# A decode step of attention plus a bilinear GLU: three filler matmuls taken out, a fourth one shortened

## The chip, the cores and the metric

The kernel runs on one core of one Trainium2 chip. The metric is the device time of one execution in microseconds; lower is better. A measurement is the median of several executions, and beside it stands one execution taken by the hardware profiler, from which all the rows below come.

## The reference

One token for each of two batch entries (B = 2, D = 512) goes through a layer norm, and then through two branches whose results are added to the input:

```python
W = min(4096, max(256, Sk // 4))            # 2048 of 8192 cached positions
q = (x @ wq).reshape(B, Sq, Hq, Dh)         # 32 heads of 128, Sq = 1
scores = einsum("bhqd,bhkd->bhqk", q, k) * Dh ** -0.5
o = einsum("bhqk,bhkd->bhqd", softmax(scores), v)
A = o.reshape(B, Sq, Hq * Dh) @ wo
Bm = ((x @ w_gate) * (x @ w_up)) @ w_down   # F = 1376, no nonlinearity
return x + A + Bm                           # x in A and Bm is the normed input
```

All is fp32. The last 2048 positions of the two caches are 32 heads x 2 x 2048 x 128 x 2 x 4 bytes = 134 MB, and every weight is read once too; the profile counts 159.5 MB of reads.

## The kernel before, in words

The host lays all inputs out in one stream, in the order in which the kernel uses them. `blocks()` writes that order down: a first small load, then steps of up to 31 x 512 columns by 128 partitions. A step goes by one DMA into one of three buffers (`BUFS = 3`, tile `step`). `pump()` issues the next load as soon as one of the buffers is free, and `done()` counts down the fields of a buffer and calls `pump()` when the last one has been used. All loads are issued on SyncE (SP). The last ones are smaller. One holds the keys of head 31, the values of head 28 with their rows of `wo`, and two blocks of `w_down` (4864 KB). The next two go into one buffer: the values of head 29 with half of those of head 31, `vh 0` (3328 KB), and the values of head 30 (2304 KB). The last four go into another buffer: the other half of head 31's values, `vh 1` (1024 KB); `wo` of head 31 with three blocks of `w_down` (1024 KB); one block of `w_down` and three half blocks (640 KB); and the last half block (128 KB). A load is told as landed as a whole.

A head h goes through these steps, each on the engines named:

- `products(h)`: VectorE multiplies the keys (128 x 8192 in two batch entries, 4096 in each access) by the query, in place in the buffer.
- `sums(h)`: VectorE sums them into the scores; then `maxima(h)` on VectorE and GpSimd.
- `weights(h)`: ScalarE takes the exponentials; GpSimd sums them over the partitions. `reciprocals(h)` on VectorE.
- `pv([h])`: TensorE multiplies the weights `p` with the values in the buffer, into the PSUM tile `o_ps`, in four groups of columns; ScalarE copies the result into `o_sb` (`copy_out`).
- `transpose([h], o_sb)`: eight small matmuls into the PSUM tile `tr`; ScalarE scales the result into `oT`.
- `project_o(h)`: TensorE multiplies `oT` with `wo`, into the accumulator `acc`.

The order on each engine is the order in which the kernel's text issues the instructions (`InOrder` fixes it), and it is written by hand from head 28 on. `down(n)`, `down_half(c, n)` are the parts of the second matmul of the GLU and also add to `acc`. Before head 28 is projected, the accumulator is copied to SBUF once (`acc_sb`, VectorE), and `accumulate(carry, acc_sb)` puts it back into PSUM in another layout, four groups of columns wide.

In this last part stand matmuls whose result is never read. `keep_busy(n)` multiplies a constant with n columns of another constant into a spare PSUM tile, `spare`. In the loop over heads 28 and 29 there are three more, which read the products of head 29 from the buffer. In the trace all of these write the tile `q`, from whose pool `spare` is taken. In fp32 a matmul stands in the trace as two MATMUL records and two LDWEIGHTS records. The TensorE's operations go through one helper and therefore carry one line number, L126; they are told apart by their tiles and shapes.

With H = 32: `HF` is head 28, and "the sums of heads 25 to 27" of the change are the `project_o` calls of the loop over `range(H - 7, HF)`.

Of the kernel before, what the change touches and what calls it, by code (L numbers as in the profile page):

```python
# [21 lines left out]
FB = 4 * P  # L22
# [10 lines left out]
GC = HG * DH  # L33
# [108 lines left out]
def kernel(  # L142
# [27 lines left out]
    tiles, used, left, got = {}, {}, {}, {}  # L170
# [46 lines left out]
    mean_w = const.tile([P, P], F32, name="mean_w")  # L217
# [87 lines left out]
    def products(h):  # L305
        g, hh = divmod(h, HG)
        kt = k_of(h)
        qb = q_ps[g][:, :, hh * DH : (hh + 1) * DH] if h else q_first
        dve.tensor_tensor(
            kt, kt, qb.unsqueeze(2).to_broadcast([P, B, J, DH]), op=ALU.mult  # L310
        )

    def sums(h):
        s_t[h] = small.tile([P, B, J], F32, name="s")
        dve.tensor_reduce(s_t[h], k_of(h), axis=AX.X, op=ALU.add)
        done("k", h)

    def maxima(h):
        s = s_t[h]
        m = small.tile([P, B], F32, name="m")  # L320
        dve.tensor_reduce(m, s, axis=AX.X, op=ALU.max)
        mm = small.tile([P, B], F32, name="mm")
        nc.gpsimd.partition_all_reduce(mm, m, P, bass_isa.ReduceOp.max)  # L323
        mm_t[h] = mm

    def weights(h):
        s, mm = s_t.pop(h), mm_t.pop(h)
        nm = small.tile([P, B], F32, name="nm")
        act.mul(nm, mm, -SCALE)
        p_t[h] = p_ring[h % NP]  # L330
        rs = small.tile([P, B], F32, name="rs")
        for b in range(B):
            act.activation(
                p_t[h][:, b, :, 8 * side(h) + 4 * b : 8 * side(h) + 4 * b + 4],
                s[:, b, :].rearrange("p (i r) -> p i r", r=4),
                AF.Exp, bias=nm[:, b : b + 1], scale=SCALE, accum_out=rs[:, b : b + 1],
            )
        sum_t[h] = small.tile([P, B], F32, name="sum")
        nc.gpsimd.partition_all_reduce(sum_t[h], rs, P, bass_isa.ReduceOp.add)  # L339

    def reciprocals(h):
        rec_t[h] = small.tile([P, B], F32, name="rec")
        dve.reciprocal(rec_t[h], sum_t.pop(h))
# [10 lines left out]
    def keep_busy(n):  # L354
        pe.matmul(spare[:, 0:n], mean_w, spare_in[:, 0:n], start=True, stop=True)
# [42 lines left out]
    def project_o(h):  # L398
        wo = got["wo", h][0]
        if h < HF:  # L400
            pe.matmul(acc, oT.pop(h), wo, start=(h == 0), stop=False)
        else:
            accumulate(oT.pop(h), wo)
        done("wo", h)
# [114 lines left out]
    spare = ps_q.tile([P, B, GC], F32, name="q")[:, 0, :]  # L519
    for h in (H - 4, H - 3):  # L520
        products(h)
        if h == H - 3:
            for i in range(3):
                pe.matmul(
                    spare, mean_w, got["k", h][0][:, i * FB : (i + 1) * FB], start=True, stop=True
                )
        sums(h)
        maxima(h)
        weights(h)
        reciprocals(h - 1)  # L530

    h = H - 2
# [5 lines left out]
    keep_busy(256)  # L538
    for i in range(H - 7, HF):
        project_o(i)  # L540
    for n in (GC, GC, 256):
        keep_busy(n)
    maxima(h)
    reciprocals(h - 1)
    products(h + 1)
# [144 lines left out]
```

## Time and profile before

| | us |
|---|---|
| median of 3 executions | 379.3 |
| lowest, highest | 379.0, 380.2 |
| the profiled execution | 379.05 |
| its span, first to last instruction | 377.2 |
| mean granted TensorE clock in it | 0.824 |
| busy: TensorE / VectorE / ScalarE | 257.0 / 295.4 / 57.4 |
| moved by DMA: mean rate over the span | 423 GB/s |

The profiled execution lies 0.25 us below the median, and 379.05 - 377.2 = 1.85 us of it lie outside its span. Times in rows of the trace count from the start of the span. A TensorE row of the timeline merges neighbouring records of one kind; its second number reaches to the modelled end of the last one, while the start of the next row tells when the next kind began. The granted clock (PEclk) is 1.00 at full speed.

### The profile page before, as it was taken

To read this page: it belongs to the slowest core of one execution; us is meant where nothing else is said; L and a number is where in the kernel's file an instruction comes from. 1 tells how busy PE (TensorE), PEld (TensorE's weight loads), DVE (VectorE), ACT (ScalarE), POOL (GpSimd) and SP (SyncE) were. 2 spreads that over 40 slices of the span, in tenths; PEclk is the share of its full clock that TensorE was granted. 3 is DMA by queue.
4 is the path that set the end of the run, shared out by engine and by line. 5 is a ranking of instruction groups with operands and counts; after the bars stand their busy time and mean duration, and the time that the engine had idled before them with its cause. 6 is when DMAs were issued, how large, how long until landed. Compare 5 with 4: busy or idle time off the path is not lost.

```text
span 377.2 us, 2895 instructions
## 1 busy us (share of the span) xinstructions
PE 257.0 (68%) x1106; PEld 89.0 (24%) x1106; DVE 295.4 (78%) x145; ACT 57.4 (15%) x260; POOL 25.3 (7%) x74
## 2 busy tenths in 40 slices
PE   3167795888586852786768706886628674759996
PEld 3133122222222220222222202231202220223243
DVE  4069999369989379999279999793899999999550
ACT  1002011110210210021012002111100210202131
POOL 1000000001010000000000000000000000000010
PEclk9999697598586996688968955898766988679999
DMA  8999999999999999999999999999999999999993
GB/s 342 430 462 464 423 405 442 431 431 432 433 431 438 431 431 431 433 431 431 438 433 438 438 431 451 431 433 431 431 431 438 426 431 431 431 415 456 405 420 151
DMA packets 3938, 159.74 MB, mean 423 GB/s; under 512 B 441, under 2 KB 697, under 8 KB 982
## 3 DMA queue, kind: packets, MB, share of 16 engines
q1 hardware_dynamic: 3926, 159.58, 98.0%
q8 instruction: 8, 0.13, 0.1%
q14 instruction: 4, 0.03, 0.0%
HBM read 159.51 MB, written 0.07 MB: 423 GB/s over the span
## 4 chain that ended last, share of the span: by engine, by line
DMA 60%; PE 20%; DVE 18%; ACT 1%; issue 1%; SPq 0%; DVEq 0%
DMA step<-in_stream_dram 60%; DVE step L126 9%; DVE s L126 8%; PE q L126 7%; PE o_ps L126 6%; PE acc L126 4%; PE tr L126 3%; ACT o_sb L126 1%; ACT oT L126 0%; DVE m L126 0%; SPq L126 0%; DVE o_out L126 0%; DVE rec L126 0%; DVEq L126 0%
## 5 line engine op out<-in xcount | busy, mean ns | idle before, releaser
L126 DVE TENSOR_TENSOR step<-step,q 128x4096 f32<-128x4096 f32 x31 | 136.8, 4412 | 44.3 <-DMA step<-in_stream_dram 38.4
L126 DVE TENSOR_REDUCE s<-step 128x32 f32<-128x4096 f32 x32 | 141.4, 4419 | 1.1
L126 PE MATMUL o_ps<-step,p 128*16 128x512 f32 x512 | 77.3, 663 | 42.7 <-DMA step<-in_stream_dram 42.7
L126 PE MATMUL q<-step,xnb 128*128 128x512 f32 (+1 forms) x128 | 76.2, 742 | 33.6 <-DMA step<-in_stream_dram 33.6
L126 PEld LDWEIGHTS q<-step,xnb 128*128 128x128 f32 x128 | 28.9, 242 | 84.1 <-issue 68.6
L126 PE MATMUL acc<-step,oT 128*2 128x512 f32 (+1 forms) x88 | 36.3, 572 | 8.6 <-ACT oT L126 8.6
L126 PE MATMUL tr<-first,o_sb 128*128 128x2 f32 (+4 forms) x192 | 29.3, 271 | 16.9 <-ACT o_sb L126 11.8
L126 PEld LDWEIGHTS tr<-first,o_sb 128*128 128x128 f32 (+2 forms) x192 | 26.7, 213 | 42.4 <-ACT o_sb L126 35.2
L126 ACT COPY o_sb<-o_ps 128x512 f32<-128x512 f32 x23 | 13.5, 586 | 149.3 <-PE o_ps L126 149.3
L126 PEld LDWEIGHTS o_ps<-step,p 128*16 128x16 f32 x512 | 13.6, 100 | 95.3 <-DMA step<-in_stream_dram 50.1
L323 POOL PARTITION_ALL_REDUCE mm<-m x32 | 11.5, 359 | 239.4 <-DVE rec L126 137.3
L126 ACT ACTIVATE nm<-mm 128x2 f32<-128x2 f32 x32 | 6.6, 205 | 125.9 <-POOL mm L323 125.9
L339 POOL PARTITION_ALL_REDUCE sum<-rs x32 | 12.8, 400 | 100.6 <-ACT p L126 100.6
L126 ACT ACTIVATE p<-s,nm 128x16 f32<-128x16 f32 x64 | 19.2, 300 | 1.0
L126 PE MATMUL o_ps<-step,xn 128*2 128x512 f32 (+1 forms) x48 | 13.7, 630 | 5.4 <-DMA step<-in_stream_dram 5.4
L126 ACT ACTIVATE oT<-tr,rec 128x1 f32<-128x1 f32 x64 | 12.1, 260 | 27.7 <-PE tr L126 27.7
L126 DVE TENSOR_TENSOR step<-step,tr 128x4096 f32<-128x4096 f32 x1 | 4.4, 4421 | 15.0 <-DMA step<-in_stream_dram 15.0
L126 ACT ACTIVATION_READ_ACCUMULATOR p<-s,nm 128x1 f32 x64 | 11.9, 186 | 0.0
L126 PEld LDWEIGHTS acc<-step,oT 128*2 128x2 f32 x88 | 4.2, 86 | 20.7 <-ACT oT L126 12.1
L126 DVE RECIPROCAL rec<-sum 128x2 f32<-128x2 f32 x32 | 5.0, 155 | 4.9 <-POOL sum L339 4.9
L126 PE MATMUL q<-xnb,mean_w 128*128 128x512 f32 (+4 forms) x24 | 8.7, 465 | 0.0
L126 PE MATMUL q<-step,mean_w 128*128 128x512 f32 x6 | 5.5, 1083 | 4.3 <-DVE step L126 4.3
(42 smaller groups left out, 48.8 us busy)
## 6 DMA issues: line engine op xcount, KB each, us to landing
step<-in_stream_dram SPq DMA_DIRECT2D x15, 7936.0 KB, 30.9
step<-in_stream_dram SPq DMA_DIRECT2D x1, 7808.0 KB, 38.8
step<-in_stream_dram SPq DMA_DIRECT2D x1, 7680.0 KB, 20.9
step<-in_stream_dram SPq DMA_DIRECT2D x1, 7552.0 KB, 57.7
step<-in_stream_dram SPq DMA_DIRECT2D x1, 4864.0 KB
step<-in_stream_dram SPq DMA_DIRECT2D x1, 3328.0 KB, 17.7
step<-in_stream_dram SPq DMA_DIRECT2D x1, 2304.0 KB, 22.8
step<-in_stream_dram SPq DMA_DIRECT2D x2, 1024.0 KB, 15.7
```

The lines of the kernel that those rows point to most:

```text
L126: made = call(*args, **kwargs)
L323: nc.gpsimd.partition_all_reduce(mm, m, P, bass_isa.ReduceOp.max)
L339: nc.gpsimd.partition_all_reduce(sum_t[h], rs, P, bass_isa.ReduceOp.add)
```

## The change

The three `keep_busy` calls (512, 512 and 256 columns) between the projections of heads 25 to 27 and the maxima of head 30 are taken out. Of the three matmuls on head 29's products, the third has 320 columns in place of 512.

```diff
     for h in (H - 4, H - 3):
         products(h)
         if h == H - 3:
-            for i in range(3):
+            for i, n in enumerate((FB, FB, 320)):
                 pe.matmul(
-                    spare, mean_w, got["k", h][0][:, i * FB : (i + 1) * FB], start=True, stop=True
+                    spare[:, :n], mean_w, got["k", h][0][:, i * FB : i * FB + n],
+                    start=True, stop=True,
                 )
         sums(h)
         maxima(h)
...
     keep_busy(256)
     for i in range(H - 7, HF):
         project_o(i)
-    for n in (GC, GC, 256):
-        keep_busy(n)
     maxima(h)
     reciprocals(h - 1)
     products(h + 1)
```

## The prediction, as it was made before any run

> **What bounds the kernel now.** I read the page first, for the whole span.
>
> ```profile
> DMA  8999999999999999999999999999999999999993
> ```
>
> The 16 DMA engines are busy in every slice but the last, so up to some 370 us the loads set the time, and only what TensorE (PE) and VectorE (DVE) do after the last loads can be shortened. Both edits lie there. I went on to the chain that ended last, and to PE's timeline from 340 us on.
>
> ```profile
> 349.42 2.67 PE acc L126 x6
> 352.08 2.35 PE q L126 x6
> ```
>
> ```profile
> 352.01 2.42 PE L126 MATMUL q<-xnb,mean_w 128*128 128x512 f32 x6
> 354.36 1.91 PE L126 MATMUL o_ps<-step,p 128*16 128x512 f32 x16
> 356.09 1.88 PE L126 MATMUL acc<-step,hT 128*2 128x512 f32 x4
> 357.90 1.05 PE L126 MATMUL tr<-first,o_sb 128*128 128x2 f32 x8
> ...
> 359.85 0.40 PE L126 MATMUL acc<-o_sb,first 2*2 2x128 f32 x8
> ...
> 360.50 1.45 PE L126 MATMUL q<-xnb,mean_w 128*128 128x512 f32 x4
> 361.88 1.91 PE L126 MATMUL o_ps<-step,p 128*16 128x512 f32 x16
> ...
> 367.43 1.91 PE L126 MATMUL o_ps<-step,p 128*16 128x512 f32 x16
> ...
> 369.79 1.05 PE L126 MATMUL o_ps<-step,p 128*16 128x512 f32 x8
> ...
> 371.55 1.05 PE L126 MATMUL tr<-first,o_sb 128*128 128x4 f32 x8
> 372.53 0.84 PE L126 MATMUL acc<-step,hT 128*2 128x128 f32 x24
> ...
> 373.63 0.85 PE L126 MATMUL acc<-step,hT 128*2 128x128 f32 x40
> ```
>
> The chain runs through the three fillers (352.08, six records of tile q, 2.35 us) straight into the value matmuls of head 28. No row here names an idle time: from 352 to the end at 373.63 + 0.85 = 374.5 every step starts when PE is through with the one before. So the last 22 us are bound by PE, and PE does 2.35 us there for nobody. What can catch it is the loads.
>
> ```profile
> 342.12 0.33 SPq L126 DMA_DIRECT2D step<-in_stream_dram  x1
> step<-in_stream_dram SPq DMA_DIRECT2D x1, 3328.0 KB, 17.7
> 342.50 0.43 SPq L126 DMA_DIRECT2D step<-in_stream_dram  x1
> step<-in_stream_dram SPq DMA_DIRECT2D x1, 2304.0 KB, 22.8
> 352.11 0.33 SPq L126 DMA_DIRECT2D step<-in_stream_dram  x1
> step<-in_stream_dram SPq DMA_DIRECT2D x1, 1024.0 KB, 15.7
> ```
>
> These are the SyncE issues, each with the row of the DMA view that has its size and its time to landing. Head 29's values land at 342.12 + 17.7 = 359.8, head 30's at 365.3, the second half of head 31's at 352.11 + 15.7 = 367.8. Between the first two, 2304 KB took 5.5 us. By that rate the load before the first of these (head 31's keys, head 28's values) landed 3328 / 2304 x 5.5 = 7.9 us before 359.8, at 351.9, and the last three (1024, 640 and 128 KB: 2.4, 1.5 and 0.3 us) land at about 370.2, 371.8 and 372.1. These four are estimates from the three landings that the rows give. PE uses each of them about 2 us after its landing: 354.36, 361.88, 367.43, 369.79. Only those 2 us can be had.
>
> **The change, part by part.** *The three fillers out.* They are 2 x (512 + 512 + 256) columns in six records; from 352.01 to 354.36 is 2.35 us, all on PE's chain. Head 28's values (351.9) are there when the projections end at 352.0, so they start at once, at 352.05: 2.3 us earlier. `down(1)`, 356.09, comes to 353.8 and ends at 355.5. Beside it runs VectorE:
>
> ```profile
> 352.11 4.42 DVE L126 TENSOR_TENSOR step<-step,q 128x4096 f32<-128x4096 f32 x1 [2.40 <-PE acc L126]
> 358.07 0.68 DVE L126 COPY o_sb<-acc 2x512 f32<-2x512 f32 x1 [1.54 <-PE acc L126]
> 358.68 4.40 DVE L126 TENSOR_REDUCE s<-step 128x32 f32<-128x4096 f32 x1
> ```
>
> The products of head 31 start at 352.11, with the landing; the view names PE, whose projections end at the same moment, and if it is PE they come no later. They end at 356.53, and the copy of the accumulator then idles 1.54 us for `down(1)`. That stall goes: the copy runs 356.55 to 357.2, the sums of head 31 from 357.2 to 361.6, and head 31's weights come 1.45 us earlier than now. On PE the carry (359.85) would come 2.3 us earlier, at 357.5, just when the copy is there. The next fillers start at 358.1 and end at 359.3; then PE waits 0.6 us for head 29's values, and starts them at 359.9, **2.0 us earlier** than 361.88. From there everything keeps 2.0 us: head 30's values at 365.45 against a landing of 365.3, head 31's second half at 367.8 against 367.8, transposes 369.6, `down(2)` 370.55 against 370.2. Head 31's weights, needed by PE at 363.8, come within 0.1 us of it. `down(3)` and the half blocks would start at 371.65 and wait for 371.8 and 372.1; the forty records now take 373.63 to 374.5, of which those behind 371.8, some 0.85 us, and the last eight behind 372.1 remain. So PE ends at about 372.75, not 374.5: **1.75 us**. The 0.6 us between 2.35 and that are given to the loads.
>
> *The shorter filler.* Its cost is read where it runs.
>
> ```profile
> 335.55 5.46 PE L126 MATMUL q<-step,mean_w 128*128 128x512 f32 x6 [4.27 <-DVE step L126]
> 338.24 0.34 PEld L126 LDWEIGHTS q<-step,mean_w 128*128 128x128 f32 x1 [0.52 <-issue]
> 339.10 0.34 PEld L126 LDWEIGHTS q<-step,mean_w 128*128 128x128 f32 x1 [0.52 <-issue]
> ```
>
> A record of 512 columns takes 339.10 - 338.24 = 0.86 us here, where the clock is at half; 192 columns less in two records are 2 x 0.86 x 192/512 = 0.64 us. The value matmuls of heads 25 to 27 follow without a gap, so 0.64 us more of them run at half speed, and from 341.1 on PE is 0.32 us ahead. In the end this buys nothing: at 352 it is 0.3 us more of waiting for the load at 351.9. The SP issues that wait for these projections (352.11) move up 0.3 us, into a queue that needs 15.7 us to get to them. At nothing, then, as long as the clock holds; if it does not, the price is the next part's.
>
> **The clock** is the cover to doubt. The steps of the granted clock lie on a grid of 3.41 us. I asked for the grid's stretches: PE busy first, PEclk third from the end; below them the same for the transposes alone (tile tr), which stream 2 to 4 columns per record.
>
> ```profile
> 252.36:255.78 3.42, 2.21 (x15) 1.23 (x12) 3.39 (x2) 1.30 (x5) 0.00 (x0) 1.00 0.95 411
> 255.78:259.19 3.41, 3.41 (x5) 0.86 (x4) 2.12 (x3) 0.73 (x5) 0.36 (x1) 0.50 1.07 465
> 269.43:272.84 3.41, 2.49 (x11) 1.35 (x12) 3.38 (x2) 0.78 (x3) 0.00 (x0) 1.00 1.03 447
> 272.84:276.26 3.42, 2.85 (x4) 0.67 (x2) 3.39 (x4) 0.81 (x5) 0.36 (x1) 0.50 0.98 427
> 327.46:330.87 3.41, 2.52 (x12) 1.22 (x12) 3.38 (x2) 1.05 (x5) 0.00 (x0) 1.00 1.12 484
> 330.87:334.28 3.41, 0.41 (x1) 0.00 (x0) 3.41 (x3) 0.89 (x5) 0.76 (x2) 1.00 0.90 391
> 334.28:337.70 3.42, 2.15 (x3) 1.15 (x4) 3.38 (x2) 0.00 (x0) 0.00 (x0) 0.50 1.03 446
> 337.70:341.11 3.41, 3.41 (x8) 0.85 (x11) 2.98 (x4) 0.44 (x3) 0.36 (x1) 0.50 0.74 318
> 344.52:347.94 3.42, 2.92 (x29) 1.34 (x22) 3.39 (x2) 1.00 (x3) 0.00 (x0) 1.00 0.89 380
> ```
>
> ```profile
> 252.36:255.78 3.42, 1.05 (x8) 0.97 (x8) 0.00 (x0) 0.72 (x4) 1.00 0.95 411
> 269.43:272.84 3.41, 1.05 (x8) 0.97 (x8) 0.00 (x0) 0.41 (x2) 1.00 1.03 447
> 327.46:330.87 3.41, 1.06 (x8) 0.97 (x8) 0.00 (x0) 0.72 (x4) 1.00 1.12 484
> 344.52:347.94 3.42, 1.17 (x9) 1.08 (x10) 0.00 (x0) 0.41 (x2) 1.00 0.89 380
> ```
>
> Busy less transposes is 1.16 us in the stretch at 252.36, and the next one ran at 0.50. At 269.43 it is 1.44, and the next ran at 0.50 too. At 327.46 it is 1.46, and the next one still had 1.00. So with about 1.45 us of real streaming in 3.41 the clock holds. At 344.52 it is now 1.75; with PE 0.32 us ahead, 0.32 us of value matmuls leave this stretch at its front and only transposes come in at its back: 1.43, on the edge. The stretches after 351 have fewer fillers but are refilled by real work: two transposes of 1 us and 0.6 us of waiting at most leave over 1.8 us in each.
>
> The Trainium skill, TensorE: Matmul & The Clock Gate, section "HAM oscillation — how this bites in real kernels", gives the rule that no idle gap of PE may be longer than about 3.4 us; by it the clock holds here, with gaps under 1 us, the slow rival below would have no chance, and the time would be the forecast's. The trace disagrees with it: the stretch at 252.36 lost the clock with 2.21 of 3.42 us busy.
>
> **The rivals.** *(1) The fillers filled a wait (0.20).* In this execution the stretch 334.28 to 337.70, busy for 2.15 us, did not wake the clock, and the next one, busy throughout, did. On a grid that lies a little otherwise it wakes a stretch earlier, and PE is up to 1.7 us ahead at 352. Then the fillers run while PE would wait for the load of 351.9, and taking them out gives 2.35 - 1.7 = 0.65 us, or 0.4 to 0.9: 378.4 to 378.9, say 378.7. For it: one profile cannot tell whether the grid always lies so. Against: the three times, 379.0 to 380.2, show none that is 1 us faster than the profiled one.
>
> *(2) The clock falls: slower (0.25).* The place is the stretch that ends at 347.94; it decides at about 1.45 us of streaming there, and the forecast is 1.43. From 347.94 the rest of the transposes, one filler of 256 columns and the three projections (2.67 us in the chain) run at half speed. Each stretch at 0.50 costs PE 3.41 / 2 = 1.7 us. One such stretch still leaves a gain of 2.67 - 1.7, capped by the loads: about 1 us. Two cost 3.4 against 2.67: +0.7 us, 380.0 from the median. A third, since value matmuls that wait for loads stream less, makes it +2.4 us, 381.7. For it: the edge above. Against: a grid elsewhere moves the two transposes into different stretches, and three projections at half speed fill a stretch and wake the clock.
>
> **How the numbers follow.** Made against the profiled execution: 379.05 - 1.75 = 377.3; its own time is 0.25 below the median, so the forecast is 377.5 for the median, with a range of its own from 377.0 to 378.1 (loads 0.5 us earlier or later). Chances: forecast 0.55, rival 1 0.20, rival 2 0.25. About 0.3% (1.1 us) is what a measurement of this kernel can tell from no change. The forecast is faster by more than that; rival 1 is within; of rival 2 one fifth (two cold stretches, +0.7) is within and the rest I count as slower, since a lost clock tends to stay lost while loads are waited for: faster 0.55, same 0.25, slower 0.20. The range reaches from 376.9 to 380.4, where the third cold stretch is left out.
>
> **What would show it.** Right: no q records between the last projection of heads 25 to 27 and the 16 o_ps records; those start at about 352.05; the copy of acc has no idle time before it; a wait of about 0.6 us for a DMA before head 29's values; PEclk 1.00 from 341 on; last TensorE record at 372.7. Wrong: 0.50 in any stretch after 344, head 28's values starting later than 354.4, or PE ending over 1 us after the last load although it started early.

## The result and the profile after

The changed kernel takes 377.50 us (median of six executions, 377.22 to 377.63) against 379.11 for the kernel before (six executions beside it, 378.5 to 380.2): a ratio of 0.9955, 95% interval 0.9941 to 0.9970, or 1.6 us. The profiled execution took 377.56 us, 1.49 less than the profiled one before. The head of the page, with the span and the DMA shares of its slices:

```profile
span 375.8 us, 2883 instructions
DMA  8999999999999999999999999999999999999995
```

There are twelve instructions fewer, six MATMUL and six LDWEIGHTS, and the loads still fill every slice but the last. The chain that ended last no longer has records of tile q between the sums of heads 25 to 27 and the value matmuls of head 28:

```profile
348.44 4.36 PE acc L126 x6
352.81 1.72 PE o_ps L126 x16
```

TensorE's timeline (start, length, what, count, and in brackets an idle time with what ended it), most of the rows that stood in the prediction:

```profile
348.37 4.43 PE L126 MATMUL acc<-step,oT 128*2 128x512 f32 x6
352.35 2.17 PE L126 MATMUL o_ps<-step,p 128*16 128x512 f32 x16
354.36 1.88 PE L126 MATMUL acc<-step,hT 128*2 128x512 f32 x4
...
358.12 0.40 PE L126 MATMUL acc<-o_sb,first 2*2 2x128 f32 x8
...
358.77 1.45 PE L126 MATMUL q<-xnb,mean_w 128*128 128x512 f32 x4
360.23 1.91 PE L126 MATMUL o_ps<-step,p 128*16 128x512 f32 x16
...
365.77 1.91 PE L126 MATMUL o_ps<-step,p 128*16 128x512 f32 x16
...
368.14 1.05 PE L126 MATMUL o_ps<-step,p 128*16 128x512 f32 x8
...
370.88 0.84 PE L126 MATMUL acc<-step,hT 128*2 128x128 f32 x24
371.53 0.62 PE L126 MATMUL acc<-step,oT 128*2 128x128 f32 x16
372.14 0.85 PE L126 MATMUL acc<-step,hT 128*2 128x128 f32 x40
```

Against these, the landings, from the issues and the time each load took to land:

```profile
340.88 0.33 SPq L126 DMA_DIRECT2D step<-in_stream_dram  x1
step<-in_stream_dram SPq DMA_DIRECT2D x1, 3328.0 KB, 19.3
341.25 0.43 SPq L126 DMA_DIRECT2D step<-in_stream_dram  x1
step<-in_stream_dram SPq DMA_DIRECT2D x1, 2304.0 KB, 24.4
352.84 0.33 SPq L126 DMA_DIRECT2D step<-in_stream_dram  x1
step<-in_stream_dram SPq DMA_DIRECT2D x1, 1024.0 KB, 15.2
```

Head 29's values land at 360.2 and are used at 360.23; head 30's land at 365.65 and are used at 365.77; the second half of head 31's land at 368.05 and are used at 368.14. The kernel before used each of them some 2 us after its landing. That distance is what the change took, and it is now down to 0.1 us: faster TensorE work could start these steps no more than that earlier. TensorE's own work from the first of these uses to the second, 5.54 us, is as long as the 5.47 us between their landings, so these rows name no wait there.

VectorE, with the stall in front of the copy of the accumulator gone:

```profile
352.39 4.42 DVE L126 TENSOR_TENSOR step<-step,q 128x4096 f32<-128x4096 f32 x1 [2.37 <-DMA step<-in_stream_dram]
356.73 0.67 DVE L126 COPY o_sb<-acc 2x512 f32<-2x512 f32 x1
357.33 4.40 DVE L126 TENSOR_REDUCE s<-step 128x32 f32<-128x4096 f32 x1
```

The releaser of head 31's products now stands as the load; in the kernel before it was put down to TensorE, which ended at the same moment.

The clock, by stretches of its grid (length, then PE busy; third from the end PEclk), and the transposes alone in the second of these stretches:

```profile
342.25:345.67 3.42, 3.42 (x36) 1.01 (x28) 3.39 (x2) 0.57 (x2) 0.19 (x1) 1.00 1.02 437
345.67:349.08 3.41, 2.91 (x19) 1.95 (x19) 3.41 (x1) 1.47 (x7) 0.00 (x0) 1.00 1.04 445
349.08:352.49 3.41, 3.41 (x8) 0.53 (x10) 1.00 (x4) 0.00 (x0) 0.35 (x1) 0.50 0.91 390
352.49:355.91 3.42, 3.42 (x21) 0.84 (x13) 3.42 (x1) 0.59 (x1) 0.00 (x0) 1.00 1.01 436
```

```profile
345.67:349.08 3.41, 1.73 (x15) 1.56 (x14) 0.00 (x0) 1.13 (x6) 1.00 1.04 445
```

In this execution the clock did fall, for one stretch, behind the one with the two transposes: the three projections took 352.35 - 348.37 = 4.0 us in place of 2.67. It cost nothing that can be seen, because they ended when the load with head 28's values came (352.39, the start of head 31's products). That they ended so early has a reason of its own: the clock had woken at 338.84, in the profile before at 341.11, and the projections began at 348.37 in place of 349.35. The shorter filler is not needed for that; in the first run below, which has it at full length, they began at 348.45. The grid also lies otherwise than in the profile before, where its edges were at 344.52 and 347.94: the difference, 1.15 us, is no whole number of stretches.

### The profile page after: what moved, and what is told of

The parts are those of the page before. It is cut to its first block, busy times and chain, and to the rows that moved or that the text cites. A ratio compares the mean times of both kernels' runs of the same rounds, so it can differ in the third digit from the quotient of the medians.

```text
span 375.8 us, 2883 instructions
## 1 busy us (share of the span) xinstructions
PE 258.1 (69%) x1100; PEld 90.0 (24%) x1100; DVE 295.3 (79%) x145; ACT 57.2 (15%) x260; POOL 25.2 (7%) x74
## 4 chain that ended last, share of the span: by engine, by line
DMA 62%; DVE 19%; PE 16%; ACT 1%; issue 1%; SPq 0%; DVEq 0%
DMA step<-in_stream_dram 62%; DVE s L126 9%; DVE step L126 9%; PE o_ps L126 5%; PE acc L126 5%; PE q L126 3%; PE tr L126 3%; ACT o_sb L126 1%; ACT oT L126 0%; DVE m L126 0%; SPq L126 0%; DVE o_out L126 0%; DVE rec L126 0%; DVEq L126 0%
## 5 line engine op out<-in xcount | busy, mean ns | idle before, releaser
L126 PE MATMUL q<-step,xnb 128*128 128x512 f32 (+1 forms) x128 | 74.6, 729 | 32.5 <-DMA step<-in_stream_dram 32.5
L126 PE MATMUL acc<-step,oT 128*2 128x512 f32 (+1 forms) x88 | 39.7, 614 | 8.6 <-ACT oT L126 8.6
L126 PE MATMUL tr<-first,o_sb 128*128 128x2 f32 (+4 forms) x192 | 31.6, 283 | 16.2 <-ACT o_sb L126 11.9
L126 PEld LDWEIGHTS tr<-first,o_sb 128*128 128x128 f32 (+2 forms) x192 | 29.0, 228 | 40.3 <-ACT o_sb L126 33.8
L126 PE MATMUL acc<-step,hT 128*2 128x128 f32 (+2 forms) x72 | 7.2, 310 | 0.0
L126 PEld LDWEIGHTS o_ps<-step,xn 128*2 128x2 f32 x48 | 2.8, 93 | 17.9 <-issue 10.7
```

Of the source, the lines that this page charges most:

```text
L126: made = call(*args, **kwargs)
```

## The experiments

Each was timed in at least five executions beside the kernel before on the same chip. The changed kernel was not timed again there, so a difference to its 377.50 us is one between two comparisons; the kernel before had medians of 378.87 to 379.11 in them. Theory L: the fillers were TensorE time on the path to the end, and behind them the loads set the limit. Against it stand S (the shorter filler has a part in it), W (the fillers filled a wait for a load, so they cost little), C and G (when the clock falls), and others named where they are tried.

**The two halves of the change alone.** First only the three fillers out; against the changed kernel:

```diff
-            for i, n in enumerate((FB, FB, 320)):
+            for i, n in enumerate((FB, FB, FB)):
```

> The three fillers are out; the third one on head 29's products keeps 512 columns. Theory L (the fillers were TensorE time on the chain, and from head 29's values on the loads set the pace): 1.6 us faster than the kernel before, 377.5, the same as the whole change. Theory S (the shorter filler has a part in it): slower than 377.5 by its 0.3 to 0.6 us, 377.8 to 378.1.

377.58 us, ratio to before 0.9960 (0.9948 to 0.9972): the whole gain. None of its five executions took longer than 377.70, and theory S, with 377.8 to 378.1, is out. Its trace, TensorE:

```profile
348.45 2.74 PE L126 MATMUL acc<-step,oT 128*2 128x512 f32 x6
352.16 1.91 PE L126 MATMUL o_ps<-step,p 128*16 128x512 f32 x16 [0.98 <-DMA step<-in_stream_dram]
...
360.04 1.91 PE L126 MATMUL o_ps<-step,p 128*16 128x512 f32 x16 [0.28 <-DMA step<-in_stream_dram]
```

Here the clock had held, and TensorE waited for both loads, 0.98 and 0.28 us. Then only the shorter filler; against the kernel before:

```diff
-            for i in range(3):
+            for i, n in enumerate((FB, FB, 320)):
```

> Only the third filler on head 29's products is cut to 320 columns; the three fillers stay. Theory L: TensorE is at most 0.3 us ahead when the clock has woken, so 378.8 to 379.1, within 0.3 us of the kernel before. Theory S: 0.6 us faster, 378.5.

378.69 us, ratio 0.9991 (0.9976 to 1.0007): not told apart from no change, but by itself not from theory S's 378.5 either. With the first run, the shorter filler carries no measurable part of the gain.

**More or less of the fillers at the same place.** One of 512 columns left in; against the changed kernel:

```diff
     for i in range(H - 7, HF):
         project_o(i)
+    keep_busy(GC)
```

> The change, with one of the three fillers (512 columns, 0.85 us at full clock) left in its place. Theory L: the changed kernel has no more than 0.2 us between the landing of head 29's values and their use, so nearly all of it comes back: 378.1 to 378.4. Theory W (a wait covers short fillers there): 377.5.

377.67 us, 0.17 above the change; ratio to before 0.9963 (0.9951 to 0.9975). Theory L's number is missed and W's comes nearer: 0.85 us of filler is nearly free. TensorE in its trace:

```profile
353.11 1.91 PE L126 MATMUL o_ps<-step,p 128*16 128x512 f32 x16
...
360.63 1.91 PE L126 MATMUL o_ps<-step,p 128*16 128x512 f32 x16
...
371.94 0.62 PE L126 MATMUL acc<-step,oT 128*2 128x128 f32 x16
372.38 0.85 PE L126 MATMUL acc<-step,hT 128*2 128x128 f32 x40
```

Head 28's values start 0.76 us later than in the changed kernel, head 29's 0.40 later, the last forty records 0.24. What shrinks on the way is head 28's value matmuls (352.35 to 354.36 in the changed kernel, where the clock was at half until 352.49, and 353.11 to 354.84 here) and a wait ahead of the last forty records (371.53 to 372.14 there, 371.94 to 372.38 here). In the first run, where the clock held, the waits of 0.98 and 0.28 us ahead of the values of heads 28 and 29 have as much room. My expectation had forgotten the wait that the prediction itself put ahead of head 29's values. So W is right for the last 0.7 us or so of the fillers, and L for what is above that. The fillers twice; against the kernel before:

```diff
-    for n in (GC, GC, 256):
+    for n in 2 * (GC, GC, 256):
```

> The kernel before, with the three fillers issued twice: 2.35 us more of TensorE at full clock at the same place. Theory L: TensorE is the bound there already, so all of it shows: 381.4. Theory W (the fillers filled a wait for a load): less than half of it, under 380.3.

381.15 us against 379.11, ratio 1.0055 (1.0041 to 1.0069): 2.04 of the 2.35 us show between the medians. In the trace the twelve records take 352.04 to 356.54, 4.50 us, so the six that were added took 2.15. In the kernel before, nearly nothing hides TensorE time at this place. The twelve records and VectorE's copy:

```profile
352.04 4.57 PE L126 MATMUL q<-xnb,mean_w 128*128 128x512 f32 x12
356.54 1.91 PE L126 MATMUL o_ps<-step,p 128*16 128x512 f32 x16
```

```profile
360.25 0.68 DVE L126 COPY o_sb<-acc 2x512 f32<-2x512 f32 x1 [3.66 <-PE acc L126]
```

Its stall grew from 1.54 to 3.66 us, in step with TensorE.

**Are the loads the limit?** The same 512 KB of columns that nothing reads were added to the load of head 29's values, in the changed kernel and in the kernel before:

```diff
-    out += [(late, v(H - 3) + [("vh", 0, CK // B)]), (late, v(H - 2))]
+    out += [(late, v(H - 3) + [("vh", 0, CK // B), ("pad", 0, 1024)]), (late, v(H - 2))]
```

> The changed kernel, with 1024 unused columns (512 KB) added to the load of head 29's values. At 2304 KB in 5.5 us that is 1.2 us of transfer, by which every later load lands later; the compute is the same. Theory L (from head 29's values on the changed kernel runs at the pace of the loads): 1.0 to 1.2 us slower than the change, 378.5 to 378.7. If TensorE's own work still sets its end: 377.5.

> The kernel before with the same 512 KB added to the same load. Theory L: TensorE uses head 29's values and all later loads some 2 us after they land, so 1.2 us later is still in time: 379.1, no more than 0.3 us slower than the kernel before. If the loads set the pace there too: 380.3.

The changed kernel with it takes 378.68 us, 1.18 more than the change (ratio to before 0.9997, 0.9986 to 1.0008, so next to nothing of the gain is left); the kernel before takes 379.11 against 378.87 for the unpadded one in the same comparison, ratio 1.0006 (0.9994 to 1.0018). Both as theory L has it, and the sharpest of the tests: the same transfer costs about its full length in one kernel and nothing that can be told in the other. Head 29's values on TensorE, in the changed kernel with the pad, 1.03 us later than without it (360.23):

```profile
361.26 1.91 PE L126 MATMUL o_ps<-step,p 128*16 128x512 f32 x16 [1.49 <-DMA step<-in_stream_dram]
```

The last forty records start 1.03 us later too (373.17). In the kernel before with the pad TensorE waits 0.16 us for head 29's values (361.43), so the pad had used up the distance there in the profiled execution.

**Is it this place, or any TensorE time?** The three fillers stay, and the next two go; against the kernel before:

```diff
-    keep_busy(GC)
-    keep_busy(192)
     o_sb = pv([H - 3])
```

> The kernel before without the two fillers (512 and 192 columns, 1.2 to 1.4 us) ahead of head 29's values; the three of the change stay. Theory L with VectorE's stall: the copy of the accumulator and the sums of head 31 are as late as before, so the weights of head 31 hold TensorE again and only some 0.5 us is gained: 378.6. If any TensorE time behind 352 us is worth the same: 1.2 to 1.4 us, 377.8.

377.81 us against 379.04, ratio 0.9976 (0.9964 to 0.9988): 1.2 us between the medians and 0.9 (0.5 to 1.4) by the ratio. The medians speak for the value of any TensorE time, against my expectation of 0.5, which the interval just leaves in. Seven of the twelve executions took 377.4 to 377.8, five 378.1 to 378.6; the trace is of the first group. In it VectorE's stall was there as said, but head 31's weights did not hold TensorE for long. VectorE, ScalarE and TensorE:

```profile
358.13 0.68 DVE L126 COPY o_sb<-acc 2x512 f32<-2x512 f32 x1 [1.62 <-PE acc L126]
363.91 0.20 ACT L126 ACTIVATE nm<-mm 128x2 f32<-128x2 f32 x1 [0.91 <-POOL mm L323]
364.60 1.05 PE L126 MATMUL o_ps<-step,p 128*16 128x512 f32 x8 [0.17 <-ACT p L126]
...
372.42 0.85 PE L126 MATMUL acc<-step,hT 128*2 128x128 f32 x40
```

TensorE waited 0.17 us for the weights, not the 0.7 to 0.9 that my expectation took off, and its last forty records start 1.21 us earlier than before (373.63). In the kernel before, ScalarE came to the weights of head 31 (nm) behind its copy of head 29's result, which had waited for TensorE:

```profile
363.86 0.59 ACT L126 COPY o_sb<-o_ps 128x512 f32<-128x512 f32 x1 [3.65 <-PE o_ps L126]
364.34 0.21 ACT L126 ACTIVATE nm<-mm 128x2 f32<-128x2 f32 x1
```

So they were late there because TensorE was, not because VectorE was; with the other fillers out ScalarE is through with its copy earlier and idles 0.91 us until GpSimd's maxima are there. What the five slower executions waited for was not traced.

**The clock.** The same two fillers out; against the changed kernel:

```diff
-    keep_busy(GC)
-    keep_busy(192)
     o_sb = pv([H - 3])
```

> The change, and the next two fillers (512 and 192 columns, between the projection of head 28 and head 29's values) are taken out too. By the loads alone (theory L) TensorE only waits 1.2 us longer for head 29's values: 377.5. Theory C (the clock holds only with some 1.45 us of streaming in a stretch of 3.41 us): the stretch with the transposes of head 28 keeps about 0.8 us of streaming, loses the clock in most executions, and one or two stretches at half speed follow: 1 to 3 us slower than the change, 378.5 to 380.5, and 0.50 in a stretch behind 358 us. Theory G (only an idle gap of over 3.4 us loses the clock): 377.5 and 1.00 to the end.

378.80 us, 1.3 above the change, in two groups: four of twelve executions at 377.2 to 377.4, eight at 378.5 to 379.2. The profiled one, at 379.03, is of the second group. TensorE, then the grid's stretches:

```profile
360.27 3.47 PE L126 MATMUL o_ps<-step,p 128*16 128x512 f32 x16 [1.66 <-DMA step<-in_stream_dram]
```

```profile
356.64:360.05 3.41, 1.96 (x22) 0.69 (x21) 3.41 (x3) 1.20 (x7) 0.40 (x1) 1.00 0.97 416
360.05:363.46 3.41, 3.19 (x16) 0.48 (x16) 1.99 (x3) 0.00 (x0) 0.36 (x1) 0.50 1.00 429
```

In this execution an idle time of 1.66 us was enough: the stretch that holds most of it had TensorE busy for 1.96 of 3.41 us, the next one ran at half speed, and head 29's value matmuls took 3.47 us in place of 1.91. Theory G is out. The Trainium skill's rule (TensorE: Matmul & The Clock Gate, "HAM oscillation — how this bites in real kernels"), "no PE-idle gaps >~3.4µs", was kept here behind 340 us and was not enough to keep the clock. Theory C has its time and its place, but not its figure: with 0.34 us of transposes in it, the stretch that lost the clock had 1.96 - 0.34 = 1.62 us of streaming, not 0.8, and that is above the 1.45 of the theory. In the run with one filler kept, a stretch with less, 2.91 - 1.56 = 1.35, did not lose it (all of TensorE, the next stretch, then the transposes alone):

```profile
344.96:348.37 3.41, 2.91 (x29) 1.65 (x21) 3.38 (x2) 1.00 (x3) 0.00 (x0) 1.00 0.95 404
348.37:351.79 3.42, 3.42 (x13) 1.11 (x13) 1.61 (x3) 0.72 (x4) 0.35 (x1) 1.00 1.01 437
```

```profile
344.96:348.37 3.41, 1.56 (x13) 1.47 (x13) 0.00 (x0) 0.41 (x2) 1.00 0.95 404
```

So a busy share well below 1 can lose the clock without a long gap, and busy time less transposes does not tell when. The four fast executions were not profiled; that the clock held in them is a reading of their times, which are theory L's. In the changed kernel these two fillers, unlike the three of the change, earn their place.

**The fillers on head 29's products**, taken out of each kernel, the whole branch (here as it stands in the kernel before):

```diff
-        if h == H - 3:
-            for i in range(3):
-                pe.matmul(
-                    spare, mean_w, got["k", h][0][:, i * FB : (i + 1) * FB], start=True, stop=True
-                )
```

> The change, and all three fillers on head 29's products are taken out. Theory C: the clock is at half when the value matmuls of heads 25 to 27 start at 340.5 us and wakes one or two stretches later; TensorE is 1 to 2 us later at 352 us, and since nothing there is spare, 378.5 to 379.5. If these fillers do nothing: 377.5.

> The kernel before, with its three fillers behind the sums of heads 25 to 27, but without the three on head 29's products. Without those the changed kernel took the same time (377.53), and its trace shows TensorE through with the projections at 352.2 us in place of about 351.2 with them, behind a clock that woke a stretch later; the load of head 31's keys hides that. In the kernel before nothing hides it, where the fillers follow the projections. Theory L: 0.5 to 1.0 us slower than the kernel before, 379.6 to 380.1. If the fillers on head 29 do nothing in either: 379.1.

Out of the changed kernel they cost nothing: 377.53 us, against my 378.5 to 379.5. Out of the kernel before they cost 1.2 us: 380.05 against 378.87, ratio 1.0027 (1.0012 to 1.0043). The first kernel's stretches, and its TensorE rows:

```profile
341.30:344.71 3.41, 3.41 (x24) 0.68 (x20) 3.41 (x1) 0.71 (x3) 0.40 (x1) 0.50 1.05 456
344.71:348.12 3.41, 3.29 (x32) 1.38 (x24) 3.38 (x2) 0.67 (x2) 0.00 (x0) 1.00 0.87 370
```

```profile
350.02 2.31 PE L126 MATMUL acc<-step,oT 128*2 128x512 f32 x5
351.96 0.62 PE L126 MATMUL o_ps<-step,p 128*16 128x512 f32 x3
```

The clock woke at 344.7; in the kernel before it was 341.1. The projections began at 350.02, 1.65 us later than in the changed kernel, but at full speed, and were all but through when head 28's values were taken up at 351.96. In the kernel before the three fillers stood between the projections and that use, and the second kernel's rows show both 1.7 us late (352.01 and 354.36 before):

```profile
353.72 2.42 PE L126 MATMUL q<-xnb,mean_w 128*128 128x512 f32 x6
356.06 1.91 PE L126 MATMUL o_ps<-step,p 128*16 128x512 f32 x16
```

So the change made one set of fillers worthless by taking out another. No version that ran is faster than the changed kernel; the one without the fillers on head 29's products equals it with fewer instructions.

## Why the prediction was right

The forecast was 377.5 us, and 377.50 was measured. The mechanism held: TensorE time was taken off the path, up to the landings of the late loads. That the numbers agree so closely is luck: the forecast took 1.8 us off a median of 379.3, and the measured difference is 1.6 us from 379.11. Point by point:

- *PE is the bound from 352 on, and its fillers are on the path.* Right, shown by the fillers alone and by the fillers twice.
- *2.3 us earlier at head 28, 2.0 us from head 29's values on, 1.75 at the end.* In the profiled execution 2.0 (354.36 to 352.35), 1.65 (361.88 to 360.23) and 1.48 (the span). Each is about 0.3 us smaller than forecast, because the loads themselves landed 0.2 to 0.4 us later in this execution (head 29's at 360.2 against 359.8); why they did is not shown. Between the medians it is 1.6 us. The mechanism, that the rest goes to the loads, is shown by the 512 KB.
- *A wait of 0.6 us ahead of head 29's values.* 0.0 in the profiled execution, 0.28 with the fillers alone out. The 0.6 was a slip in the sum: the fillers ahead of that place run from 360.50 to 361.88, and 2.3 us earlier they end at 359.6, not at 359.3. The prediction's own shifts, 2.3 us ahead of the wait and 2.0 behind it, leave 0.3 us, which the 0.28 bears out. The time did not hang on it, since the landing sets where TensorE goes on.
- *The stall of the copy goes.* It did. But head 31's weights were not within 0.1 us of holding TensorE, as the prediction had it. In the changed kernel's profile the first half of them is ready with this row of ScalarE, at 363.32, and TensorE takes it up at 364.15, 0.8 us later:

```profile
363.14 0.18 ACT L126 ACTIVATION_READ_ACCUMULATOR p<-s,nm 128x1 f32 x1
```

- *The shorter filler: nothing.* Right, as far as can be measured.
- *PEclk 1.00 from 341 on.* Wrong for the profiled execution. Rival 2's event happened, at the place that it named, and for one stretch. Its price was 1.3 us on the projections, near the 1.7 it named, but its result, a gain of only about 1 us, did not come: the projections had begun 0.98 us earlier, and the wait for the load at 352.3 took up the rest. In this the forecast was lucky for this execution. Over all six, granted clocks from 0.800 to 0.823 go with times within 0.4 us, so one stretch more or less at half speed hardly shows in the changed kernel. The bound that I drew at 1.45 us of streaming does not hold in the measure that I used: 1.18 us (2.91 - 1.73) lost the clock here and 1.62 in the run with the next fillers out, while 1.35 kept it.
- *Rival 1, the grid may lie otherwise.* The grid does move between executions, as its edges show. The Trainium skill (same page, "Part 1: The HAM clock gate") calls the window free-running, and these traces agree. In part the rival came true: TensorE was 0.98 us ahead at the projections in the changed kernel's profile, and 0.68 us (348.67) in that of the kernel before with the pad. Its argument against itself was weak: executions of the kernel before as short as 378.06 us turned up later, 1 us below the profiled one. The kernel before ranges over 1.6 to 2.7 us in a comparison and the changed one over 0.4. In the first comparison of the experiments, the six executions of the kernel before with a granted clock of 0.819 or more took 378.3 to 379.0, the five below 0.80 took 379.4 to 379.9; in the two others the relation is looser. That the grid is the reason is a reading which fits, not something that was tried by itself.

## What to carry to other kernels

A matmul that is there only to keep the clock up is worth its clock and costs its time, and both depend on what waits beside it: where the next real step waits for a load, it is free up to that wait, and where nothing is late, it is paid nearly in full. To find which, set the landing of each late load beside the first use of it; the smallest distance over the steps behind the filler is the most that its removal can bring (2.0 us here, of which 1.6 came). And do not judge the clock by the longest gap alone: it was lost behind a stretch whose longest gap was 0.50 us (the changed kernel, 345.67) and behind one with 1.66 us. Where the bound lies is not shown here.

## What was not expected of the hardware

A clock stretch at half speed in the changed kernel (3.4 us, three projections at 4.0 in place of 2.7 us) cost no measurable time, because a load landed at its end. The opposite was as large: in the profiled execution without the next two fillers, 1.66 us without work, most of it in a stretch that had 1.96 us busy, came just before the clock was lost, and the median of that kernel was 1.3 us longer.
